# Splitting the q, k and v loads over three slots and issuing them behind the slot's DMA transposes

## The chip, the cores and the metric

One core of one Trainium2 chip runs the whole program. The metric is the device time of one execution in microseconds (us), lower is better. Each kernel was run several times; the kernel before was run again on the same chip beside each test, and comparisons are made inside such a group. "Slot" means one pass of the kernel's main loop, which starts one pair of attention heads.

Engine names as in the profile: PE is TensorE (matmuls), PEld its weight loads, DVE VectorE, ACT ScalarE, POOL GpSimd, SPq the queue of the sync engine, from which nearly all DMAs of this kernel are issued.

## The reference, cut to what matters

```python
batch, n_heads, seq, head_dim = (8, 12, 448, 64)         # q, k, v
def _attn_ref(q, k, v, tau):
    q_n = q / (np.linalg.norm(q, axis=-1, keepdims=True) + 1e-06)
    k_n = k / (np.linalg.norm(k, axis=-1, keepdims=True) + 1e-06)
    scores = np.matmul(q_n, k_n.transpose(0, 1, 3, 2)) / tau
    ...                                                   # softmax
    return np.matmul(attn, v)
def _moe_ref(x, w_tok1, w_tok2, w_ch1, w_ch2):            # x: [8, 448, 768]
    xt = x.transpose(0, 2, 1)
    h = np.maximum(xt @ w_tok1, 0.0) @ w_tok2
    u = x + h.transpose(0, 2, 1)
    h2 = np.maximum(u @ w_ch1, 0.0) @ w_ch2
    return u + h2
```

There are 48 pairs of heads, 6 to a batch. Loads of the first 384 rows of q, k and v bring half a batch (three pairs, 576 KB) each; xq, xk and xv are the last 64 rows of a whole batch.

## The kernel before

In slot i the kernel computes the scores of pair i, the output of pair i-1, and the mixer of earlier pairs. From pair 15 on, the scaled k and q of pair i+2 (`qk <- kq`) and, up to pair 41, the attention output of pair i-2 (`xT <- x`) are transposed by DMA rather than on PE; the mixer's input (`ur <- ut`) is transposed by DMA for all pairs. All are issued on the sync queue, in program order, together with the loads and the stores of the output:

```python
DMA_FROM = 15
X_DMA = range(15, NP_ALL - NPAIR)
qk_at = at({n: early_qk.get(n, 3 * n - 8) for n in range(2, NHALF)})       # slot of q and k
v_at = at({n: {2: 1, 3: 5, 4: 9, 5: 11}.get(n, 3 * n - 5) for n in range(2, NHALF)})
x_at = at({b: {1: 0, 2: 6, 3: 11}.get(b, 6 * b - 8) for b in range(1, B)}) # xq and xk
xv_at = at({b: {2: 9}.get(b, 6 * b - 5) for b in range(1, B)})
...
for i in range(NP_ALL + 2):
    for n in qk_at.get(i, ()):
        load_q(n); load_k(n)
    for b in x_at.get(i, ()):
        load_xq(b); load_xk(b)
    for n in v_at.get(i, ()):
        load_v(n)
    for b in xv_at.get(i, ()):
        load_xv(b)
    if DMA_FROM <= i + 2 < NP_ALL:
        dma_tpose(i + 2)                 # qk <- kq
    if i - 2 in X_DMA:
        x_tpose(i - 2)                   # xT <- x
    for p in ut_at.get(i, ()):
        u_tpose(p)                       # ur <- ut
    ...                                  # the slot's compute, and the stores of out
```

As q and k of half n and v of half n-1 have the same slot, every third slot has all three loads, and xq and xk (or xv) with them. The user of xT is the residual of the mixer. It reads a matmul's result from a PSUM bank:

```python
psU = ps.tile([P, S], FP32, name=f"psU_{p}", tag="b")    # one of 4 banks, shared with psG, psF, psO, psX, psR
... # two matmuls into psU
nc.vector.tensor_tensor(out=ut[...], in0=psU[...], in1=xTs[p][...], op=ALU.add)   # line L367
```

## Time and profile before

| | before |
|---|---|
| time, median of 3 (lowest, highest) | 407.61 us (405.39, 407.97) |
| profiled execution | 405.75 us, span of the core 403.6 us |
| PE busy | 386.9 us, 96% |
| DVE, ACT, POOL busy | 51%, 56%, 52% |

Table of windows of the kernel before, the stretch with its largest PE gap. The columns are the window and its length in us, busy us of PE, PEld, DVE, ACT and POOL (with instruction counts), the granted share of the TensorE clock, the DMA share and GB/s:

```profile
240.00:250.00 10.00, 10.00 (x98) 5.37 (x96) 5.48 (x15) 7.42 (x15) 8.67 (x13) 1.00 0.84 215
250.00:260.00 10.00, 7.71 (x70) 4.31 (x68) 3.13 (x9) 5.95 (x10) 5.63 (x8) 1.00 1.02 194
260.00:270.00 10.00, 9.79 (x101) 5.98 (x102) 4.32 (x12) 6.33 (x12) 4.92 (x7) 1.00 0.61 113
```

PE is full on both sides and loses over 2 us in the middle. Who waits for whom (engine, line, releaser: us in total, times, longest us):

```profile
DVE ut L367 <- DMA xT<-x: 7.6, 2, 5.1
...
PE psG L385 <- DVE ut L367: 2.5, 1, 2.5
...
PE psF L399 <- ACT pt L305: 1.2, 1, 1.2
```

The first two lines are one story: a late xT holds the DVE, and the DVE holds PE. The timeline of the sync queue ahead of that gap (start us, duration us, engine, line, operation):

```profile
244.69 0.58 SPq L410 DMA_DIRECT2D out_dram<-ost  x1
245.32 0.58 SPq L106 DMA_DIRECT2D qm<-in_q_dram  x1
245.94 0.63 SPq L109 DMA_DIRECT2D km<-in_k_dram  x1
246.62 0.85 SPq L117 DMA_DIRECT2D xq<-in_q_dram  x1
247.51 4.02 SPq L124 DMA_DIRECT2D xk<-in_k_dram  x2
251.57 1.89 SPq L112 DMA_DIRECT2D vm<-in_v_dram  x1
253.57 2.10 SPq L261 DMA_TRANSPOSE qk<-kq  x1
255.77 1.21 SPq L331 DMA_TRANSPOSE xT<-x  x1
```

The timeline of DVE and PE where they were released:

```profile
259.47 0.69 DVE L367 TENSOR_TENSOR ut<-psU,xT 128x64 f16<-128x64 f32 x2 [5.11 <-DMA xT<-x]
260.21 1.31 PE L385 MATMUL psG<-ut,wc1t 128*128 128x448 f16 x6 [2.50 <-DVE ut L367]
```

The issues of six loads, 8 us of them, stand ahead of a transpose that takes 1.2 us to issue.

### The profile page before, as it was taken

Reading aid. Unit: us, or ns where it says so; the run is one execution under the profiler, and the core shown is the slowest. Engines: PE = TensorE matmul, PEld = TensorE weight load, DVE = VectorE, ACT = ScalarE, POOL = GpSimd, SP = SyncE. Lnnn points to the kernel's source line nnn. Section 1 sums busy time; section 2 is a strip of 40 time slices with the busy share of each in tenths; the row PEclk is TensorE's granted clock in tenths of the full one; section 3 lists DMA queues with packets and bytes.
Section 4 is the critical chain, followed back from the end, with each engine's and each line's share of the span. In section 5 each row is a group of like instructions: output and inputs, shape, how many; then the busy total and the mean of one; then the engine's idle time right before and its main releaser. Section 6 shows DMA issues by size and latency. Waiting matters only on the chain.

```text
span 403.6 us, 9117 instructions
## 1 busy us (share of the span) xinstructions
PE 386.9 (96%) x3646; PEld 227.6 (56%) x3646; DVE 204.7 (51%) x463; ACT 225.6 (56%) x407; POOL 208.7 (52%) x306
## 2 busy tenths in 40 slices
PE   8799999998999999999999999799999999999995
PEld 3366465575555565566555655366555565565562
DVE  5698789574354655355534645246534353242021
ACT  5998699623766457654666347455657426611400
POOL 4987495785392939394855809376673400000000
PEclk9699999999999999999999999999999999999999
DMA  8999999999792989999992998979842742022012
GB/s 219 280 256 256 241 237 191 237 228 202 194 200 55 271 181 214 167 234 187 229 165 57 249 178 211 172 165 228 212 88 50 141 98 67 15 67 91 2 78 78
DMA packets 137194, 67.51 MB, mean 167 GB/s; under 512 B 93184, under 2 KB 133568, under 8 KB 137152
## 3 DMA queue, kind: packets, MB, share of 16 engines
q1 hardware_dynamic: 132976, 61.36, 69.8%
q0 software_dynamic: 3632, 5.18, 7.3%
q8 instruction: 28, 0.46, 0.5%
q10 hardware_dynamic: 544, 0.39, 0.3%
q14 instruction: 14, 0.11, 0.1%
HBM read 43.38 MB, written 11.01 MB: 135 GB/s over the span
## 4 chain that ended last, share of the span: by engine, by line
PE 47%; POOL 20%; issue 17%; ACT 7%; DVE 4%; DMA 3%; SPq 2%; POOLq 0%; DVEq 0%
PE psF L399 18%; PE psG L385 13%; POOL kq L207 7%; POOL sq L176 6%; PE psO L318 4%; ACT pt L298 3%; PE psS L297 3%; PE psR L338 3%; PE psU L357 2%; POOL sqx L176 2%; POOL kq L218 2%; DMA xk<-in_k_dram 2%; POOL vt L164 1%; PE psX L304 1%; PE psO L320 1%
## 5 line engine op out<-in xcount | busy, mean ns | idle before, releaser
L298 ACT ACTIVATE pt<-psS 128x896 f16<-128x896 f32 x141 | 122.2, 916 | 66.0 <-PE psS L297 66.0
L385 PE MATMUL psG<-ut,wc1t 128*128 128x448 f16 x576 | 120.7, 353 | 2.5 <-DVE ut L367 2.5
L399 PE MATMUL psF<-wc2t,gt 128*128 128x384 f16 x672 | 116.3, 326 | 1.2 <-ACT pt L305 1.2
L387 ACT ACTIVATE gt<-psG 128x448 f16<-128x448 f32 x96 | 52.5, 547 | 76.1 <-PE psG L385 75.9
L207 POOL TENSOR_TENSOR kq<-km,rn 128x384 f16<-128x384 f32 x47 | 39.7, 844 | 101.7 <-ACT rn L200 100.5
L399 PEld LDWEIGHTS <-gt 128*128 128x128 f16 x672 | 64.2, 98 | 42.4 <-issue 2.4
L385 PEld LDWEIGHTS <-wc1t 128*128 128x128 f16 x576 | 53.1, 98 | 49.2 <-issue 4.4
L402 DVE TENSOR_TENSOR ost<-psF,ur 128x384 f32<-128x384 f32 x56 | 31.2, 557 | 80.4 <-PE psF L399 77.9
L318 PEld LDWEIGHTS <-pt 128*128 128x128 f16 x1152 | 52.9, 98 | 15.3 <-issue 3.3
L318 PE MATMUL psO<-vt,pt 128*128 128x65 f16 x1152 | 57.8, 194 | 0.1
L189 DVE TENSOR_REDUCE ssq<-sq 128x12 f32<-128x768 f32 (+1 forms) x49 | 45.2, 932 | 17.7 <-POOL sq L176 12.8
L297 PE MATMUL psS<-qk 64*128 64x448 f16 x282 | 41.2, 359 | 1.4 <-ACT pt L298 1.3
L324 DVE TENSOR_TENSOR x<-psO,rec 128x256 f16<-128x256 f32 x96 | 40.7, 424 | 3.3
L320 PE MATMUL psO<-vx,pt 128*128 128x130 f16 x192 | 42.0, 219 | 0.0
L323 DVE RECIPROCAL rec<-psO 128x4 f32<-128x4 f32 x96 | 17.2, 179 | 45.5 <-PE psO L320 45.4
L207 POOL TENSOR_TENSOR kq<-qm,rn 128x384 f16<-128x384 f32 x47 | 39.1, 831 | 0.0
L176 POOL TENSOR_TENSOR sq<-km 128x384 f32<-128x384 f32 x42 | 34.6, 825 | 2.8 <-DMA km<-in_k_dram 2.6
L367 DVE TENSOR_TENSOR ut<-psU,xT 128x448 f16<-128x448 f32 (+2 forms) x39 | 17.6, 477 | 23.6 <-PE psU L357 15.9
L338 PE MATMUL psR<-x,w1t 128*128 128x128 f16 x384 | 29.4, 219 | 0.1
L357 PE MATMUL psU<-w2t,r 128*128 128x448 f16 x96 | 25.9, 353 | 0.7 <-DVE x L324 0.4
L305 ACT ACTIVATE pt<-psX 128x448 f16<-128x448 f32 x48 | 26.5, 551 | 0.0
L176 POOL TENSOR_TENSOR sq<-qm 128x384 f32<-128x384 f32 x30 | 24.8, 826 | 0.8
(75 smaller groups left out, 325.2 us busy)
## 6 DMA issues: line engine op xcount, KB each, us to landing
vm<-in_v_dram SPq DMA_DIRECT2D x16, 576.0 KB, 6.8
out_dram<-ost SPq DMA_DIRECT2D x24, 384.0 KB, 2.9
qm<-in_q_dram SPq DMA_DIRECT2D x15, 576.0 KB, 5.5
km<-in_k_dram SPq DMA_DIRECT2D x15, 576.0 KB, 7.2
wc1t<-in_moe_w_ch_dram POOLq DMA_DIRECT2D x2, 1152.0 KB, 13.5
wc2t<-in_moe_w_ch_dram POOLq DMA_DIRECT2D x2, 1152.0 KB, 13.0
out_dram<-ost SPq DMA_DIRECT2D x8, 192.0 KB, 2.8
xq<-in_q_dram SPq DMA_DIRECT2D x7, 192.0 KB, 8.9
```

The lines of the kernel that those rows point to most:

```text
L176: eng.tensor_tensor(out=out, in0=src, in1=src, op=ALU.mult)
L189: nc.vector.tensor_reduce(out=ssqs[p // HP % 3][:, lo + 6 * a0:lo + 6 * a1], in_=sq[p][:, a0:a1].rearrange("p a g e -> p (a g) e"), axis=A ...
L207: eng.tensor_tensor(out=kqs[n % 2][:, j, a, 0:NC, :].rearrange("p c (g e) -> p g c e", g=2), in0=src, in1=_bcast_free(rn, E), op=ALU.mult)
L297: nc.tensor.matmul(psS[:, g, 0:S], qk[r, P * c:P * (c + 1)], qk[r, 512:512 + S], start=True, stop=True)
L298: nc.scalar.activation(out=pt[:, 2 * S * c:2 * S * (c + 1)].rearrange("p (g s) -> p g s", g=2), in_=psS[:, :, 0:S], func=AF.Exp, scale=inv ...
L318: nc.tensor.matmul(psO[:, mm, E1 * g:E1 * (g + 1)], pt[:, at:at + P], vt[:, 2 * j + g, c, 0:E1], start=(g == 0 and c == 0), stop=False)
L320: nc.tensor.matmul(psO[:, mm, :], pt[:, PX + lo:PX + lo + P], vx[:, j, 0:2 * E1], start=False, stop=True)
L324: nc.vector.tensor_tensor(out=xs[p][:, 2 * a:2 * a + 2, :].rearrange("p m (g e) -> p m g e", g=2), in0=o[:, :, :, 0:E], in1=_bcast_free(re ...
L338: nc.tensor.matmul(psR[:, tt, :], w1t[:, m, tt * P:(tt + 1) * P], xs[p][:, m, :], start=(m == 0), stop=(m == NC))
L385: nc.tensor.matmul(psG[:], wc1t[:, dt, ct * P:(ct + 1) * P], ut[:, dt, sp], start=(dt == 0), stop=(dt == DT - 1))
L387: nc.scalar.activation(out=gt[:, ct, sp], in_=psG[:], func=AF.Relu)
L399: nc.tensor.matmul(psF[:], gt[:, ct, lo:lo + P], wc2t[:, ct, dh * DH:(dh + 1) * DH], start=(ct == 0), stop=(ct == CT - 1))
```

## The change

Its intent: no load of a slot should stand ahead of that slot's transposes, and no slot should have to issue three loads. From slot 15 on the loads follow the transposes, and q (with xq), k (with xk) and v (with xv) get three different slots. Three loads before slot 15 move as well: q of half 7 from slot 13 to 12, v of half 6 and xv of batch 3 from 13 to 14.

```diff
-    qk_at = at({n: early_qk.get(n, 3 * n - 8) for n in range(2, NHALF)})
-    v_at = at({n: {2: 1, 3: 5, 4: 9, 5: 11}.get(n, 3 * n - 5) for n in range(2, NHALF)})
+    q_at = at({n: early_qk.get(n, 10 if n == 6 else 3 * n - 9) for n in range(2, NHALF)})
+    k_at = at({n: early_qk.get(n, 10 if n == 6 else 3 * n - 8) for n in range(2, NHALF)})
+    v_at = at({n: {2: 1, 3: 5, 4: 9, 5: 11}.get(n, 3 * n - 4) for n in range(2, NHALF)})
     x_at = at({b: {1: 0, 2: 6, 3: 11}.get(b, 6 * b - 8) for b in range(1, B)})
-    xv_at = at({b: {2: 9}.get(b, 6 * b - 5) for b in range(1, B)})
+    xq_at = at({b: {1: 0, 2: 6, 3: 11}.get(b, 6 * b - 9) for b in range(1, B)})
+    xv_at = at({b: {1: 1, 2: 9}.get(b, 6 * b - 4) for b in range(1, B)})
...
+    def loads(i):          # q, xq, k, xk, v, xv of slot i
...
         for i in range(NP_ALL + 2):
-            ...            # the loads, as above
+            if i < DMA_FROM:
+                loads(i)
             if DMA_FROM <= i + 2 < NP_ALL:
                 dma_tpose(i + 2)
             if i - 2 in X_DMA:
                 x_tpose(i - 2)
             for p in ut_at.get(i, ()):
                 u_tpose(p)
+            if i >= DMA_FROM:
+                loads(i)
```

More of the change, by code (lines that the diff above doesn't have):

```diff
@@ L467 @@
                 for p, t in tok2_slot.items()})
+    def loads(i):
+        for n in q_at.get(i, ()):
+            load_q(n)
+        for b in xq_at.get(i, ()):
+            load_xq(b)
+        for n in k_at.get(i, ()):
+            load_k(n)
+        for b in x_at.get(i, ()):
+            load_xk(b)
+        for n in v_at.get(i, ()):
+            load_v(n)
+        for b in xv_at.get(i, ()):
+            load_xv(b)
     def norm_begin(p, eq, ek):
@@ L562 @@
         for i in range(NP_ALL + 2):
-            for n in qk_at.get(i, ()):
-                load_q(n)
-                load_k(n)
-            for b in x_at.get(i, ()):
-                load_xq(b)
-                load_xk(b)
-            for n in v_at.get(i, ()):
-                load_v(n)
-            for b in xv_at.get(i, ()):
-                load_xv(b)
+            if i < DMA_FROM:
+                loads(i)
             if DMA_FROM <= i + 2 < NP_ALL:
```

## The prediction

> **What bounds the kernel.** TensorE. The page shows PE busy 386.9 us (96% of 403.6). The Trainium skill ("Trainium Kernel Development and Optimization", Performance Expectations) calls matmul busy time a bad metric, as matmuls are pipelined, so I read gaps: in 10 us windows PE is at 9.6 to 10.0 of 10 everywhere from 100 to 390 us but in 250 to 260 us, at 7.71. PE's idle time between 100 and 330 us adds up to about 3.5 us. DMA is busy (mostly 0.7 to 1.2 until 290 us) but hardly waited for.
>
> **The stall that the change aims at.** In the timeline the sync queue issues q, k, xq, two xk and v back to back from 245.3 to 253.5 us (the xk pair takes 4.02, v 1.89), and only then the slot's transposes: qk at 253.57, xT at 255.77. xT lands at about 259.4. DVE waits 5.1 us for it (in the waits: ut <- DMA xT, 7.6 us, 2 times), and PE 2.5 us for that ut (psG <- ut, once, ending at 260.2). The other wait for xT, 2.5 us, costs PE nothing. Elsewhere xT lands 1.6 to 13 us ahead of its use, latest in slots with loads.
>
> **What the change does.** Bytes and instructions stay the same. From slot 15 on q and xq go one slot earlier, k and xk stay, v and xv go one slot later, each behind the slot's transposes. That takes 3 to 8 us of load issues from in front of the transposes in every third slot, and 2 to 3 us of landing time: qk transposes behind loads land in 5.3 to 7.4 us, others mostly in 3.0 to 4.5. This agrees with the skill ("DMA: Bandwidth & Descriptors", Issuing engines are not separate DMA queues): all DMAs interleave on the same 16 engines.
>
> **What it could cost.** Loads land later. The k load of 245.9 us lands at 254.6 and is first squared on POOL at 269.2: 14.6 us to spare, of which I estimate that 2 to 6 go. v lands at 276 and is cast at 295; it moves about one slot (7.5 us). The q load waits for a buffer whose last reader is the scaling that the transpose ahead of it waits for too: no new blocking. I expect no wait on loads.
>
> **On the critical path.** Only the 2.5 us PE stall, and perhaps others like it in runs not profiled: the three times of before spread over 405.4 to 408.0. The chain of waits puts 20% on POOL and 17% on issue; I take that as one path among equals, as PE has no idle time there.
>
> **Prediction.** 407.6 (about 407.0 as a mean) less 2.5 us: 404.6 us, 8 in 10 within 402.0 to 407.6. Faster by over 2%: 0.03; within 2%: 0.95; slower by over 2%: 0.02.
>
> **What would show it.** Right: DVE's wait for xT and PE's 2.5 us wait for ut gone; no window below 9.6 there; qk transposes all landing in 3 to 5 us; the long issues of xk gone; xT's smallest lead above 3 us; no wait of POOL for qm, km or vm. Wrong: xT waits elsewhere, because a store or load stands ahead of the next slot's transposes; POOL or DVE waiting for a load; or a PE gap of another cause in place of the old.
>
> **What would make it wrong.** The stall may be specific to the profiled execution; then the gain is under 1 us. The sync queue is in order, so a transpose waiting for its input now holds loads behind it.

## The result, and the profile after

| | before | after |
|---|---|---|
| median, same group (lowest, highest) | 407.65 us (405.39, 410.64), 6 runs | 401.96 us (401.33, 402.49), 6 runs |
| ratio, 95% interval | | 0.9858, 0.9819 to 0.9898 |
| profiled execution | 405.75 us | 402.42 us |

A ratio is the mean time of one kernel's runs over that of the other's of the same rounds, so it is not quite the ratio of the two medians. The gain is 5.7 us (1.4%, so within 2% as predicted), but over twice the 2.5 us (3.0 us against the median) that was predicted, and the median lies just under the stated range. The spread shrinks from 5.3 to 1.2 us.

The windows after, same stretch and columns:

```profile
240.00:250.00 10.00, 10.00 (x97) 5.41 (x96) 4.64 (x12) 7.12 (x12) 9.85 (x15) 1.00 1.11 209
250.00:260.00 10.00, 10.00 (x92) 5.41 (x91) 4.56 (x11) 7.06 (x12) 3.76 (x6) 1.00 0.89 198
260.00:270.00 10.00, 9.88 (x107) 6.05 (x104) 5.75 (x15) 5.75 (x12) 8.30 (x12) 1.00 0.74 158
```

The waits after have no line in which anything waits for xT, none in which PE waits for ut, and instead of PE's 1.2 us on line L399 this one:

```profile
PE psF L399 <- DVE ost L402: 0.4, 1, 0.4
```

This one stands at 90 us, in interval 13 of the table below, and is not the change's: before_again1 has it too (0.6 us), after_again does not.

The sync queue after, in the slots of the same transposes:

```profile
240.86 0.57 SPq L106 DMA_DIRECT2D qm<-in_q_dram  x1
241.49 0.62 SPq L117 DMA_DIRECT2D xq<-in_q_dram  x1
242.21 0.59 SPq L409 DMA_DIRECT2D out_dram<-ost  x1
242.84 0.59 SPq L410 DMA_DIRECT2D out_dram<-ost  x1
243.55 2.43 SPq L261 DMA_TRANSPOSE qk<-kq  x1
246.07 1.21 SPq L331 DMA_TRANSPOSE xT<-x  x1
247.34 1.26 SPq L376 DMA_TRANSPOSE ur<-ut  x1
248.65 0.58 SPq L109 DMA_DIRECT2D km<-in_k_dram  x1
249.27 2.17 SPq L124 DMA_DIRECT2D xk<-in_k_dram  x2
```

The same xT is issued at 246.07 instead of 255.77 us, and the DVE instruction that needs it no longer waits for it:

```profile
255.41 0.69 DVE L367 TENSOR_TENSOR ut<-psU,xT 128x64 f16<-128x64 f32 x2 [1.76 <-PE psU L357]
```

So the predicted mechanism is there. But the sizes do not add up: the profiled execution of before was itself 2 us faster than its median, so a profile of it cannot show all that the median loses.

### Slot by slot

All compute engines run the same instructions in the same order in both kernels, so the two traces can be laid side by side. I took the start of the matmul psX of each pair and the time from one psX to the next; "interval 36" is from psX of pair 35 to psX of pair 36. The table gives how much longer an interval is than in `split_only` (below), whose intervals are the shortest of these (but for interval 38 of early_only). From interval 4 to the end (psX of the last pair to the end of the program included), all intervals not listed agree within 0.25 us in the kernels of this table.

| trace (time of that execution) | 13 | 14 | 22 | 24 | 36 | 38, 40 |
|---|---|---|---|---|---|---|
| before (405.75) | 0 | 1.35 | 0 | 0.10 | 2.67 | 0 |
| before_again2 (407.47) | 0 | 1.35 | 0 | 1.03 | 3.41 | 0 |
| before_again1 (408.88) | 0.77 | 1.35 | 0 | 1.33 | 3.73 | 0 |
| after (402.42) | 0.60 | 0 | 0 | 0 | 0 | 0 |
| after_again (401.79) | 0 | 0 | 0 | 0 | 0 | 0 |
| order_only (404.47) | 0 | 1.35 | 1.25 | 0 | 0 | 0, 0.18 |
| xt_first (404.86) | 0.59 | 1.36 | 0 | 0 | 0 | 1.19, 0 |
| late_only (404.26) | 0.42 | 1.36 | 0 | 0 | 0 | 0 |
| early_only (406.40) | 0 | 0 | 0 | 1.07 | 4.00 | -0.29, 0 |
| xv3 (404.19) | 0 | 0 | 0 | 0 | 2.86 | 0 |
| order_bank (403.78) | 0 | 0 | 0.57 | 0 | 0 | 0, 0.80 |

Everything that separates these kernels after the start of the program is in a handful of intervals. Intervals 24 and 36 are the two late xT (of pairs 20 and 32). Interval 14 is something else. Interval 13 comes in some executions of both kernels: there PE waits for DVE to have read a bank (`psF <- ost`, 0.3 to 0.6 us).

### The profile page after: what moved, and what is told of

Same layout as the page of the kernel before. It is cut to its first block, busy times and chain, and to the rows that moved or that the text cites. A ratio compares the mean times of both kernels' runs of the same rounds, so it can differ in the third digit from the quotient of the medians.

```text
span 400.2 us, 9113 instructions
## 1 busy us (share of the span) xinstructions
PE 384.7 (96%) x3646; PEld 226.7 (57%) x3646; DVE 205.3 (51%) x463; ACT 225.6 (56%) x407; POOL 209.1 (52%) x306
## 4 chain that ended last, share of the span: by engine, by line
PE 61%; POOL 13%; issue 6%; SPq 6%; ACT 5%; DMA 4%; DVE 3%; ACTq 0%; POOLq 0%; DVEq 0%
PE psF L399 21%; PE psG L385 20%; PE psO L318 5%; PE psS L297 5%; POOL kq L207 4%; POOL sq L176 4%; PE psR L338 3%; SPq L376 3%; PE psU L357 3%; ACT pt L298 3%; SPq L124 2%; PE psX L304 2%; POOL sqx L176 2%; POOL kq L218 2%; PE psO L320 2%
## 5 line engine op out<-in xcount | busy, mean ns | idle before, releaser
L399 PE MATMUL psF<-wc2t,gt 128*128 128x384 f16 x672 | 116.3, 326 | 0.4 <-DVE ost L402 0.4
L399 PEld LDWEIGHTS <-gt 128*128 128x128 f16 x672 | 64.1, 98 | 41.6 <-issue 1.7
```

What stands on the lines that cost most here:

```text
L399: nc.tensor.matmul(psF[:], gt[:, ct, lo:lo + P], wc2t[:, ct, dh * DH:(dh + 1) * DH], start=(ct == 0), stop=(ct == CT - 1))
```

## The experiments

Theory A: what costs time is the xT transpose standing behind loads, and the typical execution loses more there than the profiled one. Theory A2: there is a second, separate loss of 1.35 us in interval 14. Rivals: the missing microseconds come from elsewhere (B), the burst of loads that stands in one slot costs time also where it does not delay xT (C), the gap of interval 14 is also a DMA effect (D). A3 and E concern the clock.

### before_again1 and before_again2: the kernel before, profiled twice more

No edit.

> The kernel before, unchanged, for a second profile. The first profiled execution took 405.75 us, one of the fastest of before (median 407.65). Theory A (the stall behind the loads is worth more in typical executions than in the profiled one): an execution of 407 us or more shows several PE gaps released by an ut that waited for xT, summing to 4 us or more, against 2.5 us in the first profile. Rival B (the 2 us beyond my sum lie in the start or elsewhere): PE gaps behind xT again sum to 2.5 us or less and the other gaps are larger.

> The same kernel once more, to see how much the stall differs between executions. Theory A: the sum of PE gaps behind xT goes with the time, 1 us for 1 us. Rival B: it does not.

408.88 and 407.47 us. Waits of before_again1:

```profile
DVE ut L367 <- DMA xT<-x: 9.9, 2, 6.2
...
PE psG L385 <- DVE ut L367: 4.7, 2, 3.6
```

In the three traces of before the waits of DVE for xT sum to 7.6, 9.3 and 9.9 us, PE's gaps behind them to 2.5, 4.1 and 4.7 us, and the executions take 405.75, 407.47 and 408.88 us. Theory A holds, B falls. The step from a DVE wait to a PE delay is regular: in interval 36 waits of 5.11, 5.85 and 6.16 us cost PE 2.67, 3.41 and 3.73 us, and in interval 24 waits of 2.54, 3.47 and 3.77 us cost 0.10, 1.03 and 1.33 us. Each time PE loses 2.4 us less than DVE waits. So 2.4 us of PE work cover the wait, and beyond them every further tenth of lateness is paid in full. That is why executions that differ by 1 us in DMA timing differ by nearly 1 us twice.

### order_only: behind the transposes, but in the old slots

```diff
+            if i < DMA_FROM:
                 ...        # loads of the old slots
             dma_tpose, x_tpose, u_tpose
+            if i >= DMA_FROM:
+                ...        # loads of the old slots
```

> Old slots (q, k and v together in one slot of three), but from slot 15 on issued behind that slot's transposes. Theory A (what counts is that xT no longer stands behind loads): 402 to 403 us, nearly all of the 5.7 us gain, no DVE wait for xT. Rival C (what counts is that the burst of loads is split): 405 to 408 us, since a burst of 6 to 8 us of issues still stands ahead of the next slot's transposes.

Measured: 404.46 us against 408.52 of before, ratio 0.9925 (0.9880 to 0.9970), which lies between the ranges of A (402 to 403) and C (405 to 408). No wait for xT is left, but three waits that the whole change does not have:

```profile
DVE ost L402 <- DMA out_dram<-ost: 4.9, 2, 2.6
...
PE psX L304 <- DVE x L324: 1.4, 1, 1.4
...
PE psF L399 <- ACT pt L305: 1.2, 1, 1.2
```

The third is interval 14's (below). By the ratio about 3 us of the gain come from the order alone, by the medians 4. The burst now stands ahead of the next slot's transposes and, as one store shows that took 7.2 us from issue to landing (3.9 us in before), among the stores. The DVE waits for a store to land before it can write the output tile again; interval 22 grows by 1.25 us. That the one led to the other is read from the order of events, not tested.

### split_only: the new slots, but ahead of the transposes

```diff
-            if i < DMA_FROM:
-                loads(i)
+            loads(i)
             dma_tpose, x_tpose, u_tpose
-            if i >= DMA_FROM:
-                loads(i)
```

> New slots (q, k and v in three slots), but issued ahead of the slot's transposes. Theory A: part of the gain at most; each slot's transposes are late by only 1.2 to 3 us instead of 3 to 8, so xT still lands in time: I expect 402 to 405 us. Rival C: 402 us, all of the gain. If order alone and split alone both give all of it, either one is enough to keep the lead of xT above zero.

Measured: 401.80 us against 408.52, ratio 0.9856 (0.9817 to 0.9895): all of the gain, as rival C forecast and A at most in part. (The 1.35 us of interval 14 are in it, since this build has the early moves too.) With the split, at most two or three load issues stand ahead of the transposes. The smallest lead of an xT landing over its use is 0.97 us here, 4.28 and 5.65 us in the two traces of the whole change, zero in before. The order adds safety, but no time that these runs can show. Of the two parts of the change's title the three slots alone suffice.

### xt_first: the kernel before, with only x_tpose ahead of the loads

```diff
+            if i - 2 in X_DMA:
+                x_tpose(i - 2)
             ...            # loads of the old slots
             dma_tpose(i + 2)
-            if i - 2 in X_DMA:
-                x_tpose(i - 2)
```

> The kernel before, except that each slot's xT transpose is issued ahead of that slot's loads; qk and ur transposes stay behind them, and the slots of the loads are the old ones. Theory A: only xT's lateness cost PE time, so the gaps behind xT go and the time is 403 to 404.5 us. Rival C (the burst of loads itself costs time, through DMA contention or late qk transposes): 405 us or more, or a new PE wait on qk.

Measured: 405.14 us against 408.80, ratio 0.9915 (0.9869 to 0.9961). The stalls of intervals 24 and 36 are gone, as theory A says; a new one of 1.2 us appears in interval 38. There the weight load for the next scores waits for a qk transpose:

```profile
271.86 3.17 SPq L261 DMA_TRANSPOSE qk<-kq  x1
...
278.88 0.10 PEld L297 LDWEIGHTS <-qk 64*128 64x128 f16 x2 [1.29 <-DMA qk<-kq]
```

That transpose was issued behind the slot's loads and landed at 278.84 us, 6.98 us after the start of its issue. A new wait on qk, or 405 us and more, is what rival C forecast, and 405.14 us lies above A's range (403 to 404.5). So both hold: the late xT cost time, and with xT out of the way the burst still does, here through qk and in order_only through a store.

### early_only, late_only and xv3: where interval 14 comes from

early_only takes only the three moves before slot 15, late_only everything else, xv3 one of the three moves.

```diff
 early_only, on the kernel before: q of half 7 in slot 12, v of half 6 and xv of batch 3 in slot 14
 late_only, on the changed kernel: those three in slot 13 again
 xv3, on the kernel before:
-    xv_at = at({b: {2: 9}.get(b, 6 * b - 5) for b in range(1, B)})
+    xv_at = at({b: {2: 9, 3: 14}.get(b, 6 * b - 5) for b in range(1, B)})
```

> Only the three load moves before slot 15 (q of half 7 at slot 12, v of half 6 and xv of batch 3 at slot 14); from slot 15 on as before. In the built program this also changes one PSUM choice: the third output group of the mixer no longer takes the bank of psX of slot 14. Theory A2 (two separate causes, the xT waits worth about 4 us and this PSUM choice worth 1.2 us): PE's 1.2 us gap at about 94 us is gone, the gaps behind xT stay at 2.5 to 4.7 us; 1 to 1.3 us faster than before. Rival D (the 1.2 us gap comes from late stores or DMA and so the early moves only shift it, or the whole gain is from xT): no faster than before.

> The change from slot 15 on alone; loads of slots 12 to 14 as before, so the built program makes the same PSUM choice as before. Theory A2: no gap behind xT, but the 1.2 us gap at about 94 us is there: about 403.0 us, 1 us slower than the whole change. Rival D: 402 us, as the whole change.

> The kernel before with one move only: xv of batch 3 (two loads of 48 KB x 2) from slot 13 to slot 14. In the built program it flips the PSUM choice of slot 14. Theory A2: slot 14 takes 8.9 us instead of 10.25 (psX to psX on PE), and slots 24 and 36 still show the stalls behind xT. Rival D: slot 14 keeps its 1.2 us gap, as the loads of q and v still stand where they were.

(The psX that these texts call that of slot 14 is the one of pair 13, at the start of interval 14.)

Measured: early_only 406.12 us against 408.80, ratio 0.9930 (0.9886 to 0.9973), a gain of 2.7 us by the medians where 1 to 1.3 were expected (the interval allows 1.1 to 4.7); late_only 403.75 us in the same group, ratio 0.9874 (0.9834 to 0.9914); xv3 404.19 us in a single look. In xv3 DVE's waits for xT were 2.0 and 5.3 us; the first was covered, so interval 24 shows no stall, against my expectation. Interval 14 has its 1.35 us in every build with the old early slots and in none with any of the moved ones. The PE timeline of before there, and that of xv3, after the same instructions:

```profile
92.69 0.36 PE L362 MATMUL psU<-id,x 128*128 128x128 f16 x4
94.24 1.95 PE L399 MATMUL psF<-wc2t,gt 128*128 128x384 f16 x11 [1.19 <-ACT pt L305]
```

```profile
92.45 0.36 PE L362 MATMUL psU<-id,x 128*128 128x128 f16 x4
92.64 2.12 PE L399 MATMUL psF<-wc2t,gt 128*128 128x384 f16 x12
```

In before psF starts only when ACT has read psX; in xv3 it starts at once, though ACT read psX until 93.95 us. The built programs say why. The builder chooses one of the four PSUM banks of this pool for each tile when it lays out the program. In before it gave this psF the bank that psX of pair 13 had been written to two tiles earlier, and made the matmul wait for ACT; in xv3 (and early_only and after) it gave it another bank, freed already. In the built program the moved load changes six waits of PE's matmuls and the banks behind them, and nothing else on PE but the DMA semaphore that one later weight load watches. So these 1.35 us are not a DMA effect at all: they are a build-time choice that moving one small load happened to flip. Rival D falls: q and v stood where they were. Why the builder's choice depends on the place of a load was not examined.

### dose: one more load ahead of the two late transposes

```diff
+            if i in (22, 34):
+                load_spare(8 if i == 22 else 12)   # 576 KB into a tile that nobody reads
             if DMA_FROM <= i + 2 < NP_ALL:
                 dma_tpose(i + 2)
```

> The kernel before with one more load of 576 KB, into a tile that nobody reads, ahead of the transposes of slots 22 and 34, the two whose xT came late. Theory A: each wait for xT grows by the time of that load, 2 to 3 us, PE's gaps behind xT sum to 8 to 10 us, and the kernel takes 412 to 415 us. If the wait for xT were only a symptom beside another limit, the time would move by less than 2 us.

Measured: 410.07 us against 408.80, ratio 1.0022 (0.9968 to 1.0077). My expectation missed by some 2 to 5 us, and the time moved by less than 2 us, as it would have if the wait were only a symptom. By its time alone this run does not support theory A; its trace gives two reasons. First, the extra load did not cost the time of its bytes but of its issue, 1.64 and 1.92 us in the sync queue's timeline; and ahead of it the xk pair took 2.58 us in the second place instead of 4.02. In interval 24 DVE waited 4.8 us (in the traces of before 2.5, 3.5 and 3.8), in interval 36 it waited 5.7 us (before 5.1, 5.9 and 6.2). Second, in interval 24 the wait of 4.8 us cost PE 0.06 us. In before the matmul group psG that follows takes the bank of psU, which the waiting DVE instruction holds; in this build the builder had chosen another bank for it. So a late xT reaches PE there only through the bank of psU, not through the data of ut. In interval 36 of before, too, the built program gives the waiting psG the bank of psU. This was found by accident, but it shows the link. (In interval 36 PE lost 4.84 us, 3.3 of them the wait and the rest the slow clock of the next section.)

### early_only and dose: the clock after the gap

In two of the six profiles that have the stall of interval 36 with nothing put into it, early_only and dose, PE did not come back at full speed. Windows of early_only, with the clock as the third column from the right:

```profile
257.00:259.50 2.50, 0.37 (x11) 0.22 (x7) 0.62 (x3) 0.66 (x2) 0.00 (x0) 1.00 0.90 194
259.50:263.00 3.50, 3.37 (x11) 1.01 (x12) 1.44 (x4) 0.91 (x2) 0.00 (x0) 0.52 0.63 125
263.00:266.00 3.00, 3.00 (x34) 1.97 (x33) 0.94 (x3) 2.83 (x7) 0.43 (x1) 0.99 0.78 154
```

The granted clock was 0.5 for 3.4 us from 259.6 us, and the six matmuls of psG there started 0.37 us apart instead of 0.19. Of the 4.00 us of interval 36, 2.4 were the wait and 1.6 the slow clock. The Trainium skill ("TensorE: Matmul & The Clock Gate", Part 1: The HAM clock gate) describes a clock that is halved after about 3.4 us of idle, judged in windows that run freely; these traces agree with the halving and the 3.4 us of its duration. It came after an idle time of only 2.3 us and did not come after one of 3.6 us in before_again1, and the free-running windows can explain both. In all 14 traces the clock changes lie on a grid of 3.41 us. The grid window that ended as the clock fell held 1.16 us of PE work (by the modelled ends of the matmuls) in early_only and 1.18 us in dose, while the 3.6 us of before_again1 fall into two windows with 1.51 and 1.76 us of work. From 30 us on, every window with at most 1.18 us of work was followed by the slow clock (16 in all, 14 of them at the end of the program) and none of the 1500 with 1.48 us or more. (In the first 30 us windows with up to 1.75 us were followed by it too.) So here it is the place of a gap on this grid that counts, and not its length alone; no run moved a gap on purpose.

### filler: work in place of the gap

```diff
+                if i == 35:
+                    fill = ps2.tile([P, 2, 512], FP32, name="fill", tag="s")
+                    busy(fill[:, 0, :], 12)         # 12 matmuls, result unused
```

> The kernel before, with 12 matmuls of 512 columns (about 2.6 us at full clock, result unused) put just ahead of the matmul group that waits for xT in slot 36, where PE otherwise idles 2.4 to 3.7 us. Theory A3 (the idle time has a second price: after it the granted clock falls to 0.5 for 3.4 us in about half of the executions, as in the profiles of early_only and dose; 12 of 22 executions of before have a mean clock under 0.988, and those take about 2 us longer): no execution with a mean clock under 0.988, times without the upper half of before's spread, mean 0.7 to 1.2 us below before, although work was added. Rival E (the clock falls for other reasons, or costs nothing): the same share of low clocks and a time equal to before or longer.

Measured: 407.42 us against 407.54, ratio 0.9999 (0.9967 to 1.0030). The 2.75 us of added work cost nothing, which confirms that PE was idle there for another's sake: interval 36 was still 3.39 us too long, 0.63 us of them a gap after the filler. But A3's gain did not show, and its premise was wrong: two of six executions had a mean clock of 0.986, and the profile of one of them has no slow clock in the middle at all; its clock was 0.5 for 10.2 us near the start, against 6.8 us in before. The mean clock of an execution is no measure of what happens in interval 36. How often the slow clock comes there in executions not profiled, and so what it costs on average, stays open.

### after_again and order_bank

after_again has no edit; order_bank is order_only with xv3's move.

> The changed kernel unchanged, on the same chip as the others of this call, for its spread and its clocks. All theories: about 5.7 us faster than before, no execution with a mean clock under 0.988, spread under 2 us.

> As order_only, and xv of batch 3 one slot later, which makes the built program choose the other PSUM bank in slot 14. Theory A2: the parts add up: 1.35 us faster than order_only (about 403 us where before is 408.5), slot 14 as in the changed kernel, and some of 1 us left in slot 22, where the unsplit burst delays a store. Rival: 404.5 us as order_only, or 402 us (splitting has no worth of its own).

Measured in one group: after_again 401.75 us (401.65 to 402.47), ratio 0.9861 (0.9832 to 0.9889); order_bank 402.64 us, ratio 0.9884 (0.9854 to 0.9913), against 407.54 of before. The parts add up: order alone and the bank choice give all but 0.9 us (by the ratios of two groups, order_bank gains 1.7 us more than order_only), and in the profiled execution of order_bank 0.57 and 0.80 us are left in intervals 22 and 40, which the split removes.

## Why the prediction was right or wrong

- **"TensorE" bounds the kernel: right.** Outside the listed intervals the traces of the table agree within 0.25 us whatever the loads did.
- **"DVE's wait for xT and PE's 2.5 us wait for ut gone": right.** Shown by the profile after and, apart from the rest, by order_only, xt_first and late_only.
- **"407.6 (about 407.0 as a mean) less 2.5 us": the step that failed.** The 2.5 us were read from an execution of 405.75 us and taken from a median of 407.6. The mechanism was right, its size was not. Over the three traces of before the two xT intervals cost 2.77, 4.44 and 5.06 us, 4.1 on average. The text did allow for "others like it in runs not profiled", but the sum did not.
- **"On the critical path. Only the 2.5 us PE stall": wrong, a term was missing.** I began to count PE's idle time at 100 us. The 1.2 us that PE waited on line L399 stood at 94 us and in the list of waits, and I passed it over because no load was named there. Interval 14 is 1.35 us, and xv3 shows that the bank choice is its cause. The prediction also described only what happens "from slot 15 on" and left out the three moves ahead of it, which flip that choice.
- **The sum now.** Means of the three traces of before: 0.26 (interval 13) + 1.35 + 0.82 + 3.27 = 5.7 us; of the two traces of the change: 0.3 us. The difference is 5.4 us; the mean times of these executions, 407.4 and 402.1, differ by 5.3 us.
- **"I expect no wait on loads": right where the loads moved.** From 80 us on no engine waits over 0.3 us for a load. v of half 14 lands at 281.3 us and is cast at 291.7, k of that half lands at 254.0 and is used at 265.9: 11.9 us to spare, where 14.6 less 2 to 6 was estimated. New are two waits of POOL for a qk transpose to have read its source, 6.9 and 7.6 us, which cost PE nothing.
- **"qk transposes all landing in 3 to 5 us": wrong.** They take 3.0 to 6.8 us after the change; that they now meet the loads of the slot before is my reading, not tested. PE does not wait for any. **"xT's smallest lead above 3 us": right**, 5.65 us and 4.28 us.
- **"The stall may be specific to the profiled execution": the other way round.** It was smaller there than usual.

## What to carry to other kernels

Before subtracting a stall from a median, check that the profiled execution is a typical one; where it is faster than the median, its stalls may be the small ones, as here, and the spread of the times is a hint of what else is there. On a queue that issues in order, ask how many microseconds of issue stand ahead of the transfer that somebody waits for; with the same bank choice, spreading bulk loads over slots gave all of the gain here, and reordering them within a slot 0.9 us less. Putting only the late transfer first moved a part of the cost to the next transfer behind the burst. A wait of one engine on another can be a shared PSUM bank rather than data, and a small edit elsewhere can move it: compare the builds' waits before crediting an edit with a microsecond.

## What the Trainium skill lacked or had wrong

- "TensorE: Matmul & The Clock Gate" (Part 1: The HAM clock gate) ties the halved clock to an idle window of about 3.4 us, but does not say how idle the window must be. Here, from 30 us on, windows with up to 1.18 us of PE work were followed by it (early_only, dose) and windows with 1.48 us or more were not (before_again1, before_again2), so a gap of 2.3 us was enough once and one of 3.6 us was not.
- "DMA: Bandwidth & Descriptors" (Issuing engines are not separate DMA queues) calls the sequencer's issue time usually small relative to the DMA itself. Here the issues were what delayed xT: six loads took 8 us to issue, one xk pair 4.02 us behind other loads and 1.3 to 2.2 us where the loads are split, while a single load landed in 4 to 7 us (after). The same section's statement that DMAs interleave on the same engines agrees with the qk transposes of before, which take 5.1 to 7.4 us behind loads and otherwise mostly 3.0 to 4.7 us.
- No page tells that the builder's choice of a PSUM bank can put a wait between two unrelated tiles, and that it changes with an edit elsewhere. It was worth 1.35 us in interval 14 and hid a late transfer of 4.8 us in dose.
